# Batch 0 of a recurrent attention and expert kernel as one listed order of named steps

## The chip, the cores and the metric

The kernel runs on one NeuronCore of a Trainium2 chip. The metric is the device time of one execution in microseconds (us), as the median over several runs. Besides the times there is one execution taken by the hardware profiler. Engines are named as the profile names them: PE is TensorE (matmuls and transposes; PEld its weight loads), ACT is ScalarE (activations and copies), DVE is VectorE (elementwise work, reductions, 32x32 transposes), POOL is GpSimd, and SP is the queue that issues most DMAs. All arithmetic is in float32.

## The reference, cut

```python
B, H, S, Ns, D = 8, 8, 512, 32, 64          # d_model = H*D = 512, d_ff = 2048
scale = 1.0 / np.sqrt(D)
scores = scale * np.matmul(x, state.transpose(0, 1, 3, 2))    # tokens x states
a = softmax(scores)                                           # over the states
xread = np.matmul(a, state)
scores2 = scale * np.matmul(state, x.transpose(0, 1, 3, 2))   # states x tokens
a2 = softmax(scores2)                                         # over the tokens
sread = np.matmul(a2, x)
t = concatenate([xread, sread], axis=2), as rows of 512       # 8 * (512+32) rows
h = t @ w_in
sp = np.maximum(h, 0.0) + np.log1p(np.exp(-np.abs(h)))        # softplus
out = (h * erf(sp)) @ w_out
```

`softmax` stands for the subtraction of the maximum, the exponential and the division by the sum plus 1e-9. Both softmaxes use the same products of a state row and a token; only the direction of the maximum and the sum differs.

## The kernel before, in words

The token rows of `xread` are never built. For a batch, `m` = state times `w_in` per head is formed ("mixed"), and `h` = `m` transposed times `aT`, the attention weights with tokens in the free dimension. `d_ff` is cut into four groups of 512 (g = 0 to 3), each into four tiles of 128.

**Batch 0** is a hand-written sequence, because the weights arrive while it runs. `attention0` (line 297) loads `x` in natural layout, transposes it on PE (`turn`, line 308), and copies it to `xT`. The scores are then formed twice: in token layout against a block-diagonal copy of the states, `bd` (`score`, L329), and in state layout (L375). In token layout the softmax over 32 states is a reduction along the free dimension (`less`, `total`, `shared`), followed by transposes (L346) to `aT`. In state layout the softmax over tokens is `rest()` (lines 405 to 415), whose steps are taken one by one later. `warm(n)` (L194) issues n products of the identity that nothing reads.

Weights come in as raw words in 16 pieces, eight of `w_in` (kind i) and eight of `w_out` (kind o), through a pool of three `raw` buffers (line 151). A piece is converted by two ACT instructions (`on_act`, L167 and L169) and three DVE ones (`on_dve`, L172, L173, L174). After the last of them `fetch()` issues the load of the next piece. So the DVE steps set when loads start. Piece i0 is converted in two halves.

For each group, `mixed_part` (L529) forms m, `first0` (L905) h, `soft` and `erf` (L909, L912) are the two activations, `times` (L916) multiplies, and `project` (L700) accumulates the second product into four PSUM banks over all groups. In PSUM there are eight banks: two named `at`, two named `h`, and `o0` to `o3`. `states` (L210) transposes the states of batches 1 to 7. Near its end batch 0 also does the scores, softmax and mixed states of batch 1 (`attention(1)` L427, `mixed`).

**Batches 1 to 7** run in 14 stages n, each two groups of one batch. In a stage the h of one pair of groups is formed by a seven-product scheme (`hidden_wide`, L633) with pieces of the previous stage's second product between, then `project_wide` (L775) follows. Stage n = 0 is batch 1's first; it finishes batch 0's second products (eight of 64) and stores the rows. `excursion` (line 1154) is work for the next batch within a stage: the state read (`read_tokens`, L282), the next m (`mixed_pair`, L512), and the next batch's scores (L232) into the two `h` banks with their copies (L242).

**What sets the order.** Within an engine the instructions keep the order in which the program traces them: `in_order` (line 81) ties each instruction to the one before it on its engine. Between engines semaphores carry the data dependencies, which go by tile and, in PSUM, by bank. DMAs on SP are issued in traced order too; an issue waits until its buffer is free.

Of the kernel before, what the change touches and what calls it, by code (L numbers as in the profile page):

```python
# [17 lines left out]
def kernel(  # L18
# [17 lines left out]
    nc = tc.nc  # L36
# [168 lines left out]
    def states(bs, name):  # L205


        ps = ps_o.tile([P, len(bs), P], F32, name=name)
        for k, b in enumerate(bs):
            nc.tensor.transpose(out=ps[:, k], in_=st[:, b, :], identity=ident)  # L210
        return lambda: nc.scalar.copy(st[:, bs[0]:bs[-1] + 1, :], ps)

# [12 lines left out]
    def scored(b, xT, pool=ps_at, name="at"):  # L225


        s2 = [pool.tile([P, S], F32, name=name) for _ in range(2)]
# [44 lines left out]
    def read_tokens(b, a2T, z2, pool=ps_at, name="at"):  # L273
# [4 lines left out]
        for e in range(2):  # L278
            for c in range(NC):
                for i in reversed(range(NI)):  # L280
                    q = slice(Ns * i, Ns * i + Ns)
                    nc.tensor.matmul(out=sr[q, e, :], lhsT=a2T[:, e, c, q],  # L282
                                     rhs=xt[:, c, 2 * i + e, :],
                                     start=(c == 0), stop=(c == NC - 1))
        sn = sn_t[b] = const.tile([P, 2, D], F32, name="sn0") if b == 0 else \
            st[:, b - 1, :].rearrange("p (e d) -> p e d", e=2)
        for e in range(2):
# [9 lines left out]
    def attention0():  # L297

        xT = att.tile([P, H, 2, P], F32, name="xT")
        xp = [ps_o.tile([P, 2, 2, P], F32, name="o%d" % i) for i in range(NI)]
        bd = away0[:, 0:512].rearrange("p (h k n) -> p h k n", h=H, k=2)
        A = away0[:, 1024:2048].rearrange("p (g c q n) -> p g c q n", g=2, c=NC, q=NI)
        nc.vector.memset(bd, 0.0)
        on = lambda i: (nc.scalar.copy, nc.vector.tensor_copy)[i % 2]

        def turn(i, ks=range(2)):
            for k in ks:
                for e in range(2):  # L310
                    nc.tensor.transpose(
                        out=xp[i][:, e, k],
                        in_=x0[:, 2 * i + e, 2 * k:2 * k + 2].rearrange("p c d -> p (c d)"),
                        identity=ident)

        def keep_x(i):
            on(i)(xT[:, 2 * i:2 * i + 2], xp[i])

        tm, tp, aT[0] = {}, {}, keep.tile([P, 2, S], F32, name="aT")
        m1, z1 = (small.tile([P, 2, NC * NI], F32, name=n) for n in ("m1", "z1"))  # L320
        a = [A[:, g].rearrange("p c q n -> p (c q) n") for g in range(2)]
        tt = nc.vector.tensor_tensor

        def score(g, hs):
            if g not in tm:
                tm[g] = ps_at.tile([P, NC, NI, Ns], F32, name="at")
            for h in hs:
                for k in range(2):
                    nc.tensor.matmul(out=tm[g][:, 2 * k:2 * k + 2, where[h][1]],  # L329
                                     lhsT=xT[:, h, k], rhs=bd[:, h], start=True, stop=True)  # L330

        def less(g):
            t = tm[g].rearrange("p c q n -> p (c q) n")
            nc.vector.reduce_max(out=m1[:, g], in_=t, axis=AX.X)
            tt(a[g], t, over(m1[:, g]), op=ALU.subtract)
            nc.scalar.activation(out=a[g], in_=a[g], func=ACTF.Exp, scale=scale)

        def total(g):
            nc.vector.reduce_sum(out=z1[:, g], in_=a[g], axis=AX.X)
            inverse(z1[:, g])  # L340

        def shared(g):
            tt(a[g], a[g], over(z1[:, g]), op=ALU.mult)
            tp[g] = ps_o.tile([P, S], F32, name="o%d" % g)
# [982 lines left out]
```

## Time and profile before

| | |
|---|---|
| median of 3 runs | 723.47 us (723.39 to 724.16) |
| the profiled execution | 724.1 us, span 722.3 us |
| batch 0 ends, first `hidden_wide` product starts on PE | 111.42 us |
| stage n = 0, its state read starts on PE | 130.71 us |
| its `project_wide` starts on PE | 135.40 us |
| granted TensorE clock, mean | 0.999 |

Busy time of the engines in stretches of 20 us, as the view by windows gives it (stretch, length, then busy us and number of instructions of each engine, the granted clock, the DMA share and GB/s):

```profile
core 0: us, PE busy (x) PEld busy (x) DVE busy (x) ACT busy (x) POOL busy (x), PEclk, DMA share, GB/s
0.00:20.00 20.00, 18.53 (x187) 17.34 (x188) 11.39 (x23) 10.71 (x17) 0.69 (x6) 1.00 0.79 240
20.00:40.00 20.00, 19.63 (x79) 8.04 (x78) 16.16 (x19) 19.20 (x25) 0.00 (x0) 1.00 0.64 211
40.00:60.00 20.00, 19.82 (x90) 8.28 (x90) 16.24 (x19) 19.70 (x23) 0.00 (x0) 1.00 0.79 261
60.00:80.00 20.00, 20.00 (x66) 8.83 (x65) 14.09 (x20) 16.67 (x25) 0.00 (x0) 1.00 0.72 171
80.00:100.00 20.00, 20.00 (x165) 8.09 (x164) 16.64 (x25) 16.71 (x27) 0.00 (x0) 1.00 0.81 199
100.00:120.00 20.00, 18.63 (x70) 9.86 (x69) 17.23 (x27) 11.65 (x18) 0.00 (x0) 1.00 0.83 322
```

PE is busy almost throughout; from 20 to 60 us ACT is as well. A row of the timeline reads: start, duration, engine, line, operation, tiles out and in, shape, number of instructions, and in brackets the idle time before it with what ended it. A matmul's end is modelled, so the distance between two starts says more than its duration. A float32 matmul shows as two instructions, a transpose as one.

### The profile page before, as it was taken

Reading aid. Unit: us, or ns where it says so; the run is one execution under the profiler, and the core shown is the slowest. Engines: PE = TensorE matmul, PEld = TensorE weight load, DVE = VectorE, ACT = ScalarE, POOL = GpSimd, SP = SyncE. Lnnn points to the kernel's source line nnn. Section 1 sums busy time; section 2 is a strip of 40 time slices with the busy share of each in tenths; the row PEclk is TensorE's granted clock in tenths of the full one; section 3 lists DMA queues with packets and bytes.
Section 4 is the critical chain, followed back from the end, with each engine's and each line's share of the span. In section 5 each row is a group of like instructions: output and inputs, shape, how many; then the busy total and the mean of one; then the engine's idle time right before and its main releaser. Section 6 shows DMA issues by size and latency. Waiting matters only on the chain.

```text
span 722.3 us, 10976 instructions
## 1 busy us (share of the span) xinstructions
PE 714.6 (99%) x4289; PEld 565.5 (78%) x4289; DVE 538.2 (75%) x866; ACT 373.1 (52%) x540; POOL 25.2 (3%) x34
## 2 busy tenths in 40 slices
PE   9999999999999999999999999999999999999997
PEld 8444436588878878887888878887888888889996
DVE  5787879889868988788776967697877757665533
ACT  4999784636464625545346436462464535342340
POOL 0000000000100000000000000000000000000000
PEclk9999999999999999999999999999999999999999
DMA  8667795660348153513623280615242321002101
GB/s 266 193 220 211 231 273 180 148 178 30 46 89 217 21 130 55 140 51 92 98 29 147 59 140 8 175 28 148 31 103 84 89 49 27 33 29 30 24 8 30
DMA packets 144341, 74.73 MB, mean 103 GB/s; under 512 B 123424, under 2 KB 132896, under 8 KB 142752
## 3 DMA queue, kind: packets, MB, share of 16 engines
q1 hardware_dynamic: 139520, 65.95, 32.8%
q0 software_dynamic: 4032, 7.34, 7.5%
q10 hardware_dynamic: 736, 0.72, 0.3%
q8 instruction: 34, 0.56, 0.3%
q14 instruction: 19, 0.16, 0.1%
HBM read 49.87 MB, written 20.45 MB: 97 GB/s over the span
## 4 chain that ended last, share of the span: by engine, by line
PE 94%; ACT 3%; DMA 1%; DVE 0%; issue 0%; SPq 0%; ACTq 0%
PE o L775 47%; PE h L633 13%; PE at L633 10%; PE o L700 6%; PE h L678 3%; PE o L750 3%; PE h L905 2%; PE h L512 2%; PE at L512 2%; PE at L282 1%; PE h L232 1%; PE at L905 1%; PE at L529 1%; DMA x<-in_x_dram 1%; PE h L194 1%; PE at L329 1%
## 5 line engine op out<-in xcount | busy, mean ns | idle before, releaser
L775 PE MATMUL o<-w_out,ring 128*128 128x256 f32 x896 | 203.0, 379 | 0.0
L775 PEld LDWEIGHTS o<-w_out,ring 128*128 128x128 f32 x896 | 169.8, 190 | 25.0 <-DVE ring L1139 1.0
L775 PE MATMUL o<-raw,ring 128*128 128x256 f32 x672 | 161.4, 381 | 0.0
L775 PEld LDWEIGHTS o<-raw,ring 128*128 128x128 f32 x672 | 126.5, 190 | 25.9 <-ACT m L514 5.0
L626 ACT ACTIVATE ring<-ring 128x512 f32<-128x512 f32 x112 | 70.6, 631 | 59.9 <-DVE ring L616 59.3
L633 PE MATMUL h<-aT,m 128*128 128x256 f32 x336 | 82.0, 380 | 0.0
L1139 DVE TENSOR_TENSOR ring<-ring 128x1024 f32<-128x1024 f32 x60 | 70.6, 1218 | 3.9 <-ACT ring L690 3.9
L633 PEld LDWEIGHTS h<-aT,m 128*128 128x128 f32 x336 | 63.7, 190 | 10.4 <-issue 0.7
L616 DVE TENSOR_TENSOR ring<-ring,at 128x512 f32<-128x512 f32 x84 | 57.1, 680 | 16.9 <-PE at L633 15.2
L700 PE MATMUL o<-w_out,ring 128*128 128x512 f32 x128 | 58.8, 598 | 1.6 <-DVE ring L916 1.6
L760 DVE TENSOR_TENSOR ot<-uv,o 128x256 f32<-128x256 f32 (+1 forms) x56 | 30.9, 552 | 30.4 <-PE o L775 28.4
L616 DVE TENSOR_TENSOR ring<-ring,h 128x512 f32<-128x512 f32 x56 | 38.0, 678 | 19.7 <-PE h L633 19.6
L798 ACT COPY ot<-o 128x256 f32<-128x256 f32 x28 | 10.4, 373 | 79.6 <-PE o L775 79.6
L836 POOL DMA_DIRECT2D out_dram<-ot x28 | 24.5, 943 | 657.6 <-DVE ot L760 579.8
L700 PEld LDWEIGHTS o<-w_out,ring 128*128 128x128 f32 x128 | 23.7, 190 | 29.9 <-issue 24.4
L760 DVE TENSOR_TENSOR ot<-ot,o 128x256 f32<-128x256 f32 x56 | 22.1, 416 | 27.9 <-ACT ot L798 27.7
L648 ACT COPY ring<-h 128x512 f32<-128x512 f32 x28 | 16.5, 588 | 47.9 <-PE h L633 47.9
L807 DVE TENSOR_TENSOR ring<-ring 128x512 f32<-128x512 f32 x56 | 38.6, 689 | 1.4
L808 DVE TENSOR_TENSOR ring<-ring 128x512 f32<-128x512 f32 x56 | 36.3, 684 | 0.0
L639 ACT COPY ring<-h 128x512 f32<-128x512 f32 x28 | 16.5, 588 | 28.3 <-PE h L633 28.3
L690 ACT ACTIVATE ring<-ring 128x2048 f32<-128x2048 f32 x16 | 30.4, 1902 | 0.0
L514 ACT COPY m<-h 128x512 f32<-128x512 f32 x11 | 6.4, 586 | 44.4 <-PE h L512 44.3
(183 smaller groups left out, 975.6 us busy)
## 6 DMA issues: line engine op xcount, KB each, us to landing
w_in<-kept_in SPq DMA_DIRECT2D x7, 2048.0 KB, 8.2
raw<-in_moe_w_in_dram SPq DMA_DIRECT2D x16, 512.0 KB, 5.6
raw<-in_moe_w_out_dram SPq DMA_DIRECT2D x8, 1024.0 KB, 4.7
out_dram<-ot SPq DMA_DIRECT2D x32, 256.0 KB, 2.2
xq<-in_x_dram SPq DMA_DIRECT2D x112, 64.0 KB, 2.5
x<-in_x_dram SPq DMA_DIRECT2D x56, 128.0 KB, 2.9
out_dram<-ot POOLq DMA_DIRECT2D x28, 256.0 KB, 4.4
sc<-xT SPq DMA_DIRECT2D x112, 32.0 KB, 1.9
```

Source lines behind the costliest of these rows:

```text
L512: nc.tensor.matmul(out=ps[k][e][q, :], lhsT=st[r, b, q], rhs=of_group[g][r, :, i, :], start=True, stop=True)
L616: add = lambda o, x, y: nc.vector.tensor_tensor(o, x, y, op=ALU.add)
L626: nc.scalar.activation(out=s[k], in_=hs[k], func=ACTF.Softplus)
L633: nc.tensor.matmul(out=out[:, i], lhsT=x[:, q:q + P], rhs=y, start=(first and i == 0), stop=(i == 1), skip_group_check=not first)
L690: nc.scalar.activation(out=s, in_=s, func=ACTF.Erf)
L700: nc.tensor.matmul(out=acc[r], lhsT=gT[:, i, P * r:P * r + P], rhs=w_out[:, GF * g + i, :], start=(g == 0 and i == 0), stop=(g == NG - 1 a ...
L760: add = lambda o, x, y: tt(o, x, y, op=ALU.add)
L775: nc.tensor.matmul(out=out, lhsT=lhs[:, i, :], rhs=rhs[:, g, i, :], start=(start and i == 0), stop=(i == GF - 1), skip_group_check=not start)
L807: return [lambda: tt(S1, A21, A22, op=ALU.add), lambda: tt(S2, S1, A11, op=ALU.subtract), lambda: tt(S3, A11, A21, op=ALU.subtract), lambd ...
L808: lambda: tt(S3, A11, A21, op=ALU.subtract), lambda: tt(S4, A12, S2, op=ALU.subtract)]
L836: nc.gpsimd.dma_start(out=rows[2 * h + r][:, c], in_=ot[:, c], accum_op=ALU.add)
L1139: nc.vector.tensor_tensor(s[:, ks], s[:, ks], hs[:, ks], op=ALU.mult)
```

## The change

`attention0`, `first0`, `mixed_part`, `mixed` and the sequence of calls are replaced by a table `do` of named steps and one string that lists them. Three functions fill the table: `start0` (attention of batch 0), `groups0` (m, h, activations and second products) and `weights0` (the conversions); `next0` holds what batch 0 does for batch 1.

How to read the names: `x1` transposes tile 1 of x; `x1_v` and `x3_a` are its copy on DVE or ACT. `st` turns batch 0's states, `s0` and `s1` are the two halves of the scores in state layout, `s00_a` to `s11_a` their copies, `tm0`, `tm1` turn them to token layout; `max`, `less`, `exp`, `sum`, `inv`, `norm` are the softmax over states, `ta` its transposes. `big`, `wt`, `wz`, `wn`, `tw`, `read` are the softmax over tokens and the state read. `i0a0` is ACT step 0 of piece i0 (`+` its second half), `i0v2` a DVE step, `get` loads the next piece. `m10` is m of group 1 from tile 0, `m100_v` its copy; `h11` h of group 1, tile 1 (`h000`: one half of it); `soft`, `erf`, `mul` follow, and `p120` is the second product of group 1, rows 2, tile 0. `u0`, `u1` turn the other states. `lxq`, `lx` load inputs, `q`, `qm`, `qe`, `qs`, `qr`, `n`, `cm`, `ca` are batch 1's scores, softmax, m and sums, and `kept` writes the converted weights to memory.

What differs in the work itself: the scores in token layout are transposes of those in state layout and no longer products with `bd`; the token weights are divided by their sums before their transposes and no longer after the read; `warm(16)` is `warm(12)`; many copies of m are on DVE; the activations of group 1 to 3 come in another grouping with other work between; loads are issued by `get` and no longer by the last conversion step. In stage n = 0 the inner `erf` is issued between the two mixed states, both copies of one bank pair are on two engines, two of the four stores come later, and the products' multiplication is cut in two. From batch 3 on the scores go to the two `o` banks that the next `project_wide` will use.

```diff
+        def turn_st():
+            held["st"] = ps_h.tile([P, 2 * P], F32, name="h")
+            for g in range(2):
+                nc.tensor.transpose(out=held["st"][:, P * g:P * g + P],
+                                    in_=st0[:, g].rearrange("p k d -> p (k d)"), identity=ident)
+
+        def score(g):
+            if not nat:
+                nat.update({k: ps_o.tile([P, 2, 2, P], F32, name="o%d" % k) for k in range(2)})
+            for h in range(4 * g, 4 * g + 4):
+                q = slice(Ns * where[h][1], Ns * where[h][1] + Ns)
+                for c in range(NC):
+                    r = slice(D * (c % 2), D * (c % 2) + D)
+                    nc.tensor.matmul(out=nat[c % 2][q, g, c // 2],
+                                     lhsT=st00[r, Ns * h:Ns * h + Ns], rhs=xT[r, h, c // 2],
+                                     start=True, stop=True)
+
+        def turn_score(g):
+            tm[g] = ps_at.tile([P, NC, NI, Ns], F32, name="at")
+            for c in range(NC):
+                nc.tensor.transpose(out=tm[g][:, c].rearrange("p q n -> p (q n)"),
+                                    in_=sc[:, g, c], identity=ident)
...
+            do["wn%d" % e] = lambda e=e: nc.vector.tensor_scalar(
+                a2[:, e], a2[:, e], z2[:, e:e + 1], None, op0=ALU.mult)
...
+    order0 = """
+        w8 x1 x1_v i0a0 i0a1 x0 x0_v i0v0 i0+a1 i0+a0 st st_v i0v1 x2 x2_v x3 x3_a s0 s00_a i0+v0
+        i0v2 s1 i0+v1 i0+v2 s01_a s10_a tm0 max0 less0 s11_a tm1 exp0 w12 max1 less1 sum0 i1a0
+        inv0 norm0 exp1 o0a0 m01 sum1 m011_a u0 m010_a i1a1 ta0 ta0_a inv1 norm1 m00 ta1 big1
+        i1v0 m000_a get i1v1 i1v2 m001_a h000 ta1_a h01 u0_v o0v0 m02 m020_v h001 u1 m021_v h03
+        h02 o1a1 o0a1 soft01 o0v1 o0v2 u1_v lxq1 soft00 erf00+ mul00 mul01 p030 get o1a0 p020
+        o1v0 o1v1 o1v2 soft03 get p000 soft02 erf02+ mul02 i2a0 mul03 p001 i2a1 p010 i2v0 p031
+        i2v1 i2v2 p021 i3a0 i3a1 i3v0 p002 p011 get p003 o2a1 big0 big p032 o2a0 wt0 m10 m100_v
+        p012 wt1 p013 m101_v h11 soft11 h10 soft10 i3v1 i3v2 m12 m121_a xq1v wz p033 p022 wn0
+        p023 o2v0 m120_v h13 o2v1 o2v2 h12 erf10+ mul10 get o3a1 wn1 get mul11 o3a0 o3v0 o3v1
+        p110 soft13 soft12 o3v2 p111 erf12+ mul12 i4a0 i4a1 get get i5a0 p100 p101 p130 p131 p132
+        mul13 tw0 tw0_a i4v0 i5a1 i4v1 i4v2 p102 p112 m20 m201_a m200_a p120 i5v0 i5v1 p121 p122
+        h20 i5v2 o4a0 o4v0 get m22 m221_v m220_v get h21 o4a1 o4v1 o4v2 tw1 tw1_v h22 soft20 o5a0
+        o5v0 h23 p133 p123 o5a1 soft21 erf20 mul20 erf21 soft23 soft22 o5v1 mul21 p103 erf22 p200
+        o5v2 p201 p220 get erf23 mul22 mul23 i6a0 i6v0 i6a1 i6v1 read read_v p113 i7a0 i7v0 i6v2
+        p210 get get q q1_v p221 p230 qm1 o6a0 q0_a qm0 m30 o6v0 p222 o6a1 m301_v i7a1 p211
+        m300_a o6v1 o6v2 n1 n10_a n11_v qm7 cm0 h30 n0 n01_a i7v1 qm6 h31 lx1 soft31 soft30 p202
+        p203 i7v2 qm8 erf30 n00_v kept cm2 cm1 cm3 m32 m320_a p223 p231 p232 mul30 qm2 erf31 p233
+        p330 m321_a qe3 h33 qm3 mul31 lxq2 o7a0 qm4 o7v0 get get p331 h32 qe2 qm5 p300 p301 qe1
+        qs1 qe0 qs0 p320 p321 qs2 qr0 qr2 soft33 erf33 p212 qr1 p213 p310 p311 o7a1 ca0 qr3
+        soft32 erf32 ca2 mul33 ca1 ca3 o7v1 o7v2 get mul32
+    """
+    steps0 = order0.split()
+    for n, name in enumerate(steps0):
+        if n == len(steps0) - 40:
+            overlap = traced()
+        do[name]()
...
-            (nc.vector.tensor_copy if both and not k else nc.scalar.copy)(m_t[b, g][:, 0], ps[k][0])
+            nc.scalar.copy(m_t[b, g][:, 0], ps[k][0])
             (nc.vector.tensor_copy if split and not k else nc.scalar.copy)(m_t[b, g][:, 1], ps[k][1])
...
+            if k == 0:
+                then()
...
             if c is not None:
-                soft[c] = attention(c, xq_t[c].rearrange("p i m d -> p i (m d)"), ps_h, "h")
+                k = 2 * (n_acc[0] % 2)
+                banks = (ps_h, ("h", "h")) if n == 0 else (ps_o, ("o%d" % k, "o%d" % (k + 1)))
+                soft[c] = attention(c, xq_t[c].rearrange("p i m d -> p i (m d)"), *banks)
...
-        erf_part(inner, inside)
         if n == 0:
             done(steps)
-            excursion(1, (1, sets(1 - begins(1))), 2)
-        times_part(inner, outside)
+            excursion(1, (1, sets(1 - begins(1))), 2, lambda: erf_part(inner, inside))
+            for r in 2, 3:
+                do["put%d" % r]()
+        if n == 0:
+            times_part(inner, slice(0, 1))
+            times_part(inner, slice(3, 4))
+        else:
+            erf_part(inner, inside)
+            times_part(inner, outside)
         times_part(inner, inside)
```

## The prediction

> **What bounds the kernel now.** I read the page's busy shares first, then the list of waits, then the timeline of TensorE where batch 0 starts, where it ends, and where the third and fourth states are mixed.
>
> ```profile
> PE 714.6 (99%) x4289; PEld 565.5 (78%) x4289; DVE 538.2 (75%) x866; ACT 373.1 (52%) x540; POOL 25.2 (3%) x34
> PE 94%; ACT 3%; DMA 1%; DVE 0%; issue 0%; SPq 0%; ACTq 0%
> PE o L700 <- DVE ring L916: 1.6, 2, 1.4
> PE h L194 <- POOL ident masks.py:199: 1.4, 1, 1.4
> ```
>
> TensorE is the bound and nearly never idle, so a gain is either TensorE work that goes, or time that TensorE loses to others. The list of waits admits some 3 us of loss. It understates, because the end of a matmul is modelled: a late operand shows as a row whose instructions stand too far apart. So I compare start times.
>
> ```profile
> 1.36 3.79 PE L194 MATMUL h<-ident 128*128 128x128 f32 x16 [1.36 <-POOL ident masks.py:199]
> 8.49 3.76 PE L329 MATMUL at<-ring,xT 128*128 128x64 f32 x32
> 12.18 2.48 PE L375 MATMUL o<-xT,ring 64*32 64x128 f32 x64
> 14.59 3.84 PE L194 MATMUL h<-ident 128*128 128x128 f32 x32
> 18.26 0.60 PE L346 MATMUL o<-ident,ring 128*128 128x128 f32 x4
> 29.16 7.03 PE L700 MATMUL o<-w_out,ring 128*128 128x512 f32 x16
> 36.38 3.70 PE L700 MATMUL o<-w_out,ring 128*128 128x512 f32 x8 [0.19 <-DVE ring L916]
> 40.27 0.67 PE L529 MATMUL at<-w_in,ring 64*32 64x256 f32 x16 [0.18 <-DVE w_in L174]
> 49.48 9.61 PE L700 MATMUL o<-w_out,ring 128*128 128x512 f32 x22
> 59.02 0.66 PE L529 MATMUL at<-ring 64*32 64x256 f32 x16
> 85.61 2.04 PE L232 MATMUL at<-xq,st 64*32 64x512 f32 x16
> 87.58 1.98 PE L905 MATMUL h<-aT,m 128*128 128x512 f32 x4
> 98.27 3.60 PE L700 MATMUL o<-w_out,ring 128*128 128x512 f32 x8
> 103.23 1.99 PE L700 MATMUL o<-w_out,ring 128*128 128x512 f32 x4 [1.37 <-DVE ring L916]
> 105.15 1.09 PE L529 MATMUL at<-w_in,st 64*32 64x512 f32 x16
> 133.67 1.69 PE L232 MATMUL h<-xq,st 64*32 64x512 f32 x16
> 135.40 1.99 PE L775 MATMUL o<-w_out,ring 128*128 128x256 f32 x8
> 209.93 1.24 PE L232 MATMUL h<-xq,st 64*32 64x512 f32 x16
> 211.10 7.17 PE L775 MATMUL o<-w_out,ring 128*128 128x256 f32 x32
> ```
>
> From 49.48 to 59.02 stand 22 instructions, 0.434 us each: the undisturbed price (a float32 product is two). At 29.16 the 24 take 11.11 instead of 10.41: 0.7 lost. At 98.27 the 12 take 6.88 instead of 5.21: 1.67 lost. State scores take 1.17 undisturbed (209.93 to 211.10); at 85.61 they take 1.97 (0.8 lost), at 133.67 1.73 (0.56 lost). From 135 on every row stands at its price: the change can win nothing there.
>
> Two rows show who releases the start:
>
> ```profile
> 9.15 0.67 ACT L167 ACTIVATE w_in<-raw 128x512 f32<-128x512 f32 x1 [0.40 <-DMA raw<-in_moe_w_in_dram]
> 25.54 1.28 ACT L912 ACT_TABLE_LOAD   x1
> ```
>
> The first weights land at about 9.13, and ScalarE was already waiting.
>
> **What the Trainium skill says.** "TensorE: Matmul & The Clock Gate", section "What's actually happening": the array runs at half clock until it has been busy for some 3.4 us, and again after an idle window of that length. The trace agrees on the first half: the 16 warm-up products at 1.36 take 3.58 us to the next row (0.22 each), the 32 at 14.59 take 3.67 (0.115 each). No row shows a fall back. The same page, "Architectural detail", calls the ScalarE and VectorE queues strict FIFO: a step behind a late one is late too. "PSUM — Partial Sum Buffer", section "PSUM bank collisions raise a hardware error", says to guard by bank and not by address; in the changed program the copy of one half of the natural scores indeed waits for the end of both halves. "ScalarE: Activation LUTs", "What ACT_TABLE_LOAD costs": 1.28 us plus a drain of 1.38. The trace has the 1.28, but the next activation starts at 26.83, right behind the load; I use 1.28.
>
> **The change, part by part.**
>
> *TensorE work.* The 32 score instructions of L329 (3.69 us, 8.49 to 12.18) become 8 transposes of the natural scores (0.11 each by the 8 at 79.39, 0.87 us): 2.8 less. The filler warm(16) becomes warm(12): 8 of 32 instructions, 0.9 less. So 3.7 us of work goes, but all of it lies before 19 us, where TensorE waits for the softmax chain anyway (that is why the filler stood there). It counts only if the chain gets shorter.
>
> *The start, as queues.* The listed order puts four weight conversions ahead of the copies. ScalarE: i0a0 waits for the landing, 9.15 to 9.82, then i0a1, i0+a1 (second half lands about 10.5), i0+a0 to 11.78, then x3_a to 12.27. VectorE: i0v0 waits for i0a0 and st_v stands behind it, ending 10.6. So the first natural scores s0, possible at 8.5 before, start at 10.65; half of 2.41 each, s0 ends 11.85. Copy s00_a (0.37, row L367's size) ends 12.54; s1, which writes its bank, runs 12.6 to 13.8; three more copies to 14.9 (a copy starts some 0.2 behind the matmul, as in all rows); transposes tm0, tm1; max0 15.0 and less0 to 16.4 (0.69 each), exp0 to 17.1, less1 17.7, exp1 behind i1a0 18.65, norm0 19.5, sum1, inv1, norm1 21.3. ta1 and its copy end at 22.6. First product h000 stands at 22.0, against 19.71 before (L905), with m01 and u0 (0.38 + 0.53) already done.
>
> *Up to group 0's second products.* VectorE then does big1 and the three steps of i1 (0.69 + 1.23 + 1.23) to 25.1; m02 waits for them, then h001, u1, h03, h02 (0.6 + 0.87 + 0.33 + 1.75 + 1.75) end at 30.5. On ScalarE i1a1, two copies, o1a1, o0a1, a table load, two softplus, a table load and the erf end at 29.85; mul00 behind u1_v ends at 30.55. p030 starts at 30.6, where the old p started at 29.16: 1.4 late.
>
> *30 to 53.* Seven p (0.87 each) reach 36.6; mul02 is ready at 36.35 (o1a0, two loads, softplus and erf to 35.65). The 0.7 lost before at 29 to 40 is thus gone. m10 waits for i2v2 at 40.25, 0.25 lost. From there the sum of the list is: group 1's first p at 53.0, where the old kernel, at the same state (group 0 done, all h of group 1 done), stood at 52.06. So 0.95 behind.
>
> *53 to the end of batch 0.* The work left is the same. At each step I set the operand beside TensorE: mul12 57.3 for 58.15, i4v2 61.2 for 61.3, mul20 ahead by 3 us, i6v2 1.4 ahead of m30, n00_v 0.6 ahead of m32, combine_a 2 us ahead of the next stage. None is late by this sum; two are within 0.1. Added on ScalarE: five table loads more up to there (21 against 16, 6.4 us), hidden since ten copies of m (0.38 each) move to VectorE and ScalarE was free for about 3 of each 20 us after 60; without that cover each load costs 1.28. Added on VectorE: two scalings wn0, wn1 (0.42 each) for the two of L288. lxq1's 16 issues now stand on SP ahead of i2's load (0.53 each, 17 to 25.5); i2 lands by 32 and is used at 35.5. kept is issued earlier, and the 12 us of its landing no longer meet the next stage. Old stretch 52.06 to 111.42 = 59.36; less 0.8 (scores) and 1.67 (erf wait) gives 56.9; I add 0.45 for read and q standing apart and for products broken into smaller runs: 57.35. Batch 0 ends at 110.35, 1.07 earlier.
>
> *Third stage.* Before, both copies of the first mixed state were VectorE's (132.92 and 133.53, to 134.2) and the scores waited for the second. Now one is ScalarE's, ahead of the inner erf: the scores start as before and lose nothing, 0.56 gained. times(0) alone is ready 0.5 ahead of the first product. The last two puts go behind the score copies; their banks are o2, o3, the next product's o0, o1.
>
> *Scores in the o banks.* No row after 135 loses anything: 0. The banks are last read by the product before; if that cover failed, a wait of one copy (0.59) a stage.
>
> Sum: 1.07 + 0.56 = 1.63, say 1.65. Of the profiled run, 724.1 (span 722.3 and 1.8 around it), 722.45 is left; of the median 723.47, **721.8**.
>
> **Rivals.**
> *The start loses nothing* (group 1's p at 52.06 again, as the copies and landings run ahead of my sum): 0.95 more, and up to 0.3 of edges: 720.6. For: four of the steps are within 0.1 us of TensorE, so the list fits. Against: the landing at 9.13.
> *The ties break the wrong way*: i4v2 for m20, mul12 for p132, n00_v for m32 each some 0.5 late, since five more table loads stand on ScalarE: about 1.5 back, 723.3, no change.
> *The array's clock falls back* (slower). TensorE now idles 8.5 to 10.65 and is half idle to 15.5. If one window counts as idle, s0, s1 and the transposes run at half clock, 1.2 + 1.2 + 0.2 later on the chain, and warm(12) takes 5.3 instead of 2.6 and holds up ta0, 1.4: 4.0 in all, 725.8. It decides where the idle stretch gets beyond 3.4 us by the page; the sum has 2.15.
>
> **How the numbers follow.** Forecast 0.52, start without loss 0.24, ties 0.14, clock 0.10. Two runs of this kernel tell about 0.2% apart, 1.45 us: faster is below 722.0. Of the forecast's own spread (720.6 to 723.0) some 0.58 lies there: 0.30; with the first rival 0.24 and a little of the ties, 0.55. Slower is the clock and little else, 0.10; the rest, 0.35. Range 719.8 to 724.6: below, the first rival with 0.8 for copies moved at nothing; above, ties with one more table load.
>
> **What would show it.** Natural scores starting at 10.6 and h at 22 on TensorE; second products of group 0 at 30.6; no gap in their rows; the old gap of 1.4 at 103 gone; hidden products of the third stage (old 111.42) at 110.35; scores there in 1.2 us. Wrong if the first rows of TensorE after 8.5 stand at double spacing, if m20 or m32 wait, or if rows after 135 change.

## The result, and the profile after

| | before | after |
|---|---|---|
| median of 20 runs each | 724.11 us (723.23 to 724.74) | 722.90 us (721.52 to 725.67) |
| profiled execution, its span | 724.10, 722.3 us | 722.23, 720.4 us |
| batch 0 ends (first product of `hidden_wide`) | 111.42 us | 110.07 us |
| `project_wide` of the third stage starts | 135.40 us | 133.21 us |
| the last group of eight matmuls starts | 716.19 us | 714.68 us |

The ratio of after to before is 0.9985, with a 95% interval of 0.9978 to 0.9992: a gain of about 1.1 us (0.6 to 1.6), small but clear of zero. The runs of the changed kernel also spread over 4.2 us, those before over 1.5.

The small sum hides larger parts. The timeline of TensorE after the change, with start, busy time, the group and the idle time ahead of it:

```profile
9.64 0.72 PE L788 MATMUL o<-xT,ring 64*32 64x128 f32 x32 [2.29 <-DVE ring L748]
11.66 1.16 PE L788 MATMUL o<-xT,ring 64*32 64x128 f32 x32 [1.30 <-ACT ring L747]
14.94 4.25 PE L194 MATMUL h<-ident 128*128 128x128 f32 x24
19.12 0.45 PE L877 MATMUL at<-w_in,ring 64*32 64x128 f32 x16
21.86 2.84 PE L887 MATMUL h<-aT,m 128*128 128x512 f32 x6 [0.17 <-ACT m L747]
30.26 9.68 PE L894 MATMUL o<-w_out,ring 128*128 128x512 f32 x22
39.87 0.67 PE L877 MATMUL at<-w_in,ring 64*32 64x256 f32 x16
61.23 0.67 PE L877 MATMUL at<-ring 64*32 64x256 f32 x16 [0.39 <-DVE ring L174]
103.20 7.03 PE L894 MATMUL o<-w_out,ring 128*128 128x512 f32 x16
110.07 1.03 PE L489 MATMUL h<-aT,m 128*128 128x256 f32 x4
132.04 1.24 PE L224 MATMUL h<-xq,st 64*32 64x512 f32 x16
133.21 1.99 PE L631 MATMUL o<-w_out,ring 128*128 128x256 f32 x8
150.06 1.03 PE L489 MATMUL h<-aT,m 128*128 128x256 f32 x4
152.75 1.13 PE L489 MATMUL h<-aT,m 128*128 128x256 f32 x4 [1.66 <-DVE ring L472]
```

Read it by start times, as before. The 22 second products from 30.26 to 39.87 take 9.61, their price (0.437 each); the 0.7 that the old kernel lost there is gone. So is the wait of 1.67 at 98 to 105: from 103.20 the 16 products run through. The scores of the third stage take 1.17 (132.04 to 133.21) in place of 1.73. But at 150.06 there is something that the old kernel did not have: four hidden products that should take 0.86 take 2.69, until 152.75. From there to the end the changed kernel is 1.25 us shorter than the old one at the same work.

The sum, on the start times of TensorE: batch 0 -1.35, third stage -0.84, fourth stage +1.93, later stages -1.25, together -1.51; another 0.4 of the span lies behind the last matmul, and no run asks why. Of these four the forecast had the first two.

### The new wait

From the view of waits of the changed kernel, the new one of TensorE (what waited, for whom, us in total, times, longest):

```profile
PE h L489 <- DVE ring L472: 1.7, 1, 1.7
```

What VectorE did in front of that L472 (two rows of the softmax, between 149.56 and 151.36, are left out):

```profile
143.17 1.30 DVE L321 STREAM_TRANSPOSE xT<-sc 128x512 f32<-128x512 f32 x2
147.77 0.69 DVE L616 TENSOR_TENSOR ot<-uv,o 128x512 f32<-128x512 f32 x1 [3.30 <-PE o L631]
148.37 1.27 DVE L323 TENSOR_REDUCE m<-xT 128x16 f32<-128x512 f32 x2
151.36 0.74 DVE L616 TENSOR_TENSOR ot<-ot,o 128x256 f32<-128x256 f32 x2
152.02 0.68 DVE L472 TENSOR_TENSOR ring<-ring,h 128x512 f32<-128x512 f32 x1
```

It stood still for 3.30 us before the add into an output buffer `ot` at 147.77. The view names a product (PE o L631), the releaser that came last by its records. But this add takes the first eight of the 24 products that start at 142.29, and they end at their price by 144.0. What else does the add need? The buffer `ot`, one of three, and its last reader is a store. SP's queue, before the change and after it (first issue, length, what is issued, how many):

```profile
133.32 0.82 SPq L838 DMA_DIRECT2D out_dram<-ot  x2
134.23 4.53 SPq L75 DMA_DIRECT2D x<-in_x_dram  x8
138.88 9.11 SPq L102 DMA_DIRECT2D xq<-in_x_dram  x16
```

```profile
130.35 5.09 SPq L75 DMA_DIRECT2D x<-in_x_dram  x8
135.55 8.46 SPq L102 DMA_DIRECT2D xq<-in_x_dram  x16
144.12 1.85 SPq L694 DMA_DIRECT2D out_dram<-ot  x2
```

Before, the last two stores of batch 0 went out at 133.32, ahead of the 24 loads that the excursion brings. After, they are traced behind the excursion and go out behind its 24 issues: 144.12. Each lands 3.5 us after its issue, the first at about 147.65, and the add starts at 147.77. (That SP issues in traced order is tied only in batch 0: the last `in_order`, for the stages behind it, names TensorE, VectorE and ScalarE. There the trace has to show the order, as here.) That the one causes the other is argued from times so far; the first experiments test it.

### The profile page after: what moved, and what is told of

Same layout as the page of the kernel before. It is cut to its first block, busy times and chain, and to the rows that moved or that the text cites. A ratio compares the mean times of both kernels' runs of the same rounds, so it can differ in the third digit from the quotient of the medians.

```text
span 720.4 us, 10904 instructions
## 1 busy us (share of the span) xinstructions
PE 708.6 (98%) x4257; PEld 561.2 (78%) x4257; DVE 542.0 (75%) x877; ACT 374.8 (52%) x535; POOL 25.2 (3%) x34
## 4 chain that ended last, share of the span: by engine, by line
PE 89%; ACT 4%; DMA 2%; SPq 2%; DVE 2%; issue 1%; DVEq 0%; ACTq 0%
PE o L631 46%; PE h L489 13%; PE at L489 10%; PE o L894 5%; PE h L534 3%; PE o L606 3%; PE h L383 2%; PE at L383 1%; PE at L275 1%; SPq L102 1%; PE h L887 1%; ACT raw L169 1%; PE at L887 1%; DMA raw<-in_moe_w_in_dram 1%; DMA raw<-in_moe_w_out_dram 1%; SPq L75 1%
## 5 line engine op out<-in xcount | busy, mean ns | idle before, releaser
L631 PE MATMUL o<-w_out,ring 128*128 128x256 f32 x896 | 203.0, 379 | 0.0
L631 PEld LDWEIGHTS o<-w_out,ring 128*128 128x128 f32 x896 | 169.9, 190 | 24.8 <-DVE ring L1089 0.8
L631 PE MATMUL o<-raw,ring 128*128 128x256 f32 x672 | 161.4, 381 | 0.0
L631 PEld LDWEIGHTS o<-raw,ring 128*128 128x128 f32 x672 | 126.6, 190 | 25.8 <-ACT m L385 9.2
L1089 DVE TENSOR_TENSOR ring<-ring 128x1024 f32<-128x1024 f32 (+1 forms) x61 | 70.6, 1200 | 4.5 <-ACT ring L546 4.5
L472 DVE TENSOR_TENSOR ring<-ring,at 128x512 f32<-128x512 f32 x84 | 57.0, 679 | 16.8 <-PE at L489 15.2
L472 DVE TENSOR_TENSOR ring<-ring,h 128x512 f32<-128x512 f32 x56 | 38.0, 678 | 19.7 <-PE h L489 19.6
L894 PEld LDWEIGHTS o<-w_out,ring 128*128 128x128 f32 x128 | 23.6, 190 | 27.2 <-issue 24.6
L616 DVE TENSOR_TENSOR ot<-ot,o 128x256 f32<-128x256 f32 x56 | 22.1, 416 | 27.9 <-ACT ot L654 27.7
L504 ACT COPY ring<-h 128x512 f32<-128x512 f32 x28 | 16.4, 586 | 47.9 <-PE h L489 47.9
L489 PE MATMUL h<-sy,sx 128*128 128x256 f32 x112 | 28.7, 379 | 0.0
```

The lines of the kernel that those rows point to most:

```text
L472: add = lambda o, x, y: nc.vector.tensor_tensor(o, x, y, op=ALU.add)
L489: nc.tensor.matmul(out=out[:, i], lhsT=x[:, q:q + P], rhs=y, start=(first and i == 0), stop=(i == 1), skip_group_check=not first)
L616: add = lambda o, x, y: tt(o, x, y, op=ALU.add)
L631: nc.tensor.matmul(out=out, lhsT=lhs[:, i, :], rhs=rhs[:, g, i, :], start=(start and i == 0), stop=(i == GF - 1), skip_group_check=not start)
L894: nc.tensor.matmul(out=acc[r], lhsT=gT[g][:, i, P * r:P * r + P], rhs=w_out[:, GF * g + i, :], start=(made_of[r] == 1), stop=(made_of[r] = ...
L1089: nc.vector.tensor_tensor(s[:, ks], s[:, ks], hs[:, ks], op=ALU.mult)
```

## The experiments

All runs are compared with the kernel before on the same chip. Its medians there lie between 724.06 and 724.41 us, so kernels of different groups are compared by their ratios. Every kernel computes the whole output.

### What makes the fourth stage wait

Theory 1: the order on SP. Theory 2: the copies and the erf that the change puts on ScalarE in the third stage. A third is batch 0's list itself. Four kernels ran together.

**e1**, the third stage's edits taken back (the forms of the kernel before: stores at the end of each row of second products, copies of the first mixed state on VectorE, one erf ahead of the excursion, its multiplication in one instruction). 

> The changed kernel with the third stage's edits taken back: all four output blocks of batch 0 are copied and stored ahead of the scores, both copies of the first mixed state are VectorE's, the erf of the inner half stands ahead of the scores, and its multiplication is one instruction. The list of batch 0 and the score banks stay. Theory 1 (the two late stores stand on SP behind the 24 issues of the next loads, so their output buffers come free 12 us late and VectorE's add in the fourth stage waits): the stores land near 136, the wait of 1.7 us in the hidden products near 151 is gone, and the scores near 132 take 1.73 again instead of 1.17; the excess from 130 on falls by about 1.9 - 0.6 - 0.3 = 1.0, and the time is about 722.0, 0.9987 of the changed kernel's. Theory 2 (the wait comes from the copies or the erf on ScalarE): the wait goes too. A third (it comes from batch 0's list, which leaves VectorE more to do): it stays at 1.7, and the time grows by 0.6 to 0.8, to 723.6.

**e2**, only the loads move:

```diff
+            waiting.append(lambda: None)
             excursion(1, (1, sets(1 - begins(1))), 2, lambda: erf_part(inner, inside))
             for r in 2, 3:
                 do["put%d" % r]()
+            all_of(waiting)
+            waiting.clear()
```

where `load_x` and `load_xq` are put into `waiting` while it is not empty. 

> The changed kernel with one difference: in the third stage the loads of the next x and the next turned x are issued behind the two late stores instead of ahead of them; copies, erf and scores stay where they are. Theory 1 (order on SP): the two stores land near 136 instead of 148, VectorE's add with the output buffer o2 waits for nothing, the wait of 1.7 us near 151 is gone, and nothing takes its place, since the loads come only some 1.3 us later: 1.9 us less, 721.0, 0.9974 of the changed kernel's. Theory 2 (copies or erf on ScalarE): the wait stays, 722.9, a ratio of 1.000.

**e3**, only the queue of the two stores changes:

```diff
-            put_x(0, r // 2)(r % 2, ot)
+            put_x(0, r // 2)(r % 2, ot, queue=nc.scalar if r > 1 else nc.sync)
```

> The changed kernel with one difference: the two late stores of batch 0 are issued on ScalarE's queue, each behind its own copy, and SP's order of loads stays. Theory 1: as with the loads behind the stores, the wait near 151 is gone and the time is 721.0 (0.9974); what two issues take on ScalarE (not shown so far, estimated at no more than 0.1 to 0.6 us each, by SP's 0.53 a DMA) stands behind the score copies and hits the erf of the outer half, which has 2 us of room. Theory 2: the wait stays, 722.9 (1.000).

**e5**, e2 with `banks = ps_h, ("h", "h")` for all stages. 

> The loads issued behind the two late stores, as in the run of that name, and besides the scores of all later stages back in the two h banks, as before the change. The forecast said that the o banks change nothing: then this equals the run with the loads behind the stores, 721.0, and the score rows take 1.17 in both. A second reading, from the rows of the changed kernel (0.995 us for a group of 16 in the o banks, 1.165 in the h banks of the kernel before): five groups take 0.17 longer, 0.85 in all, 721.85, ratio 1.0012 to the other.

| | median, us | ratio to before, 95% | wait near 151 | third-stage scores |
|---|---|---|---|---|
| after | 722.90 | 0.9985 (0.9978 to 0.9992) | 1.93 | 1.17 |
| e1 | 721.66 | 0.9968 (0.9955 to 0.9980) | 0 | 1.73 |
| e2 | 720.11 | 0.9952 (0.9940 to 0.9965) | 0 | 1.16 |
| e3 | 720.87 | 0.9959 (0.9947 to 0.9972) | 0 | 1.17 |
| e5 | 721.97 | 0.9975 (0.9968 to 0.9983) | 0 | 1.16 |

SP's queue of e2, and the same add of VectorE there (L622 in its numbering):

```profile
131.57 5.63 SPq L75 DMA_DIRECT2D x<-in_x_dram  x8
137.31 0.44 SPq L102 DMA_DIRECT2D xq<-in_x_dram  x1
137.85 0.91 SPq L700 DMA_DIRECT2D out_dram<-ot  x2
138.81 9.18 SPq L102 DMA_DIRECT2D xq<-in_x_dram  x15
```

```profile
144.38 1.30 DVE L327 STREAM_TRANSPOSE xT<-sc 128x512 f32<-128x512 f32 x2
145.60 0.65 DVE L622 TENSOR_TENSOR ot<-uv,o 128x512 f32<-128x512 f32 x1
```

The stores pass 15 of the 16 issues of `xq` (the eight of `x` and one of `xq` still go first, though traced behind the stores: nothing ties SP's order here), and the add starts right behind the transpose, with no idle time. e3 leaves SP's order and moves only the two stores off it: the wait goes as well. Both leave the copies and the erf on ScalarE where the change put them. Theory 2 is refuted, and theory 1 shown. The third falls with e1, which keeps the list and has no wait. In e3 the two issues took 0.37 and 0.36 on ScalarE's queue, and ScalarE needed 2.09 from the first of the two copies to the next erf, in e2 0.96. 0.47 of that came back as a late product at 144.67. So e2 is the cleaner cure in the trace, though the times of the two can't be told apart. The Trainium skill, "DMA: Bandwidth & Descriptors", section "Issuing engines are not separate DMA queues", says that another queue saves only the issuer's time, usually small beside the transfer. The traces agree on what is saved, but here it wasn't small: the 24 issues ahead of the stores took SP 13.7 us, and a store landed in 3.5.

e1 shows the size of the third stage's edits without their side effect: from batch 0's end to `project_wide` it needs 23.82 us (111.13 to 134.95), e2 and the changed kernel 23.14, the kernel before 23.98. So these edits are worth 0.68 of the third stage's 0.84.

### The score banks

e5 against e2 says that the o banks are worth more than noise: 0.9975 against 0.9952, and in the traces 1.24 us between 165 and the last matmul (by start times, some 0.85 in the five score groups and 0.40 in the mixed states ahead of them). So the part was tried alone on the kernel before. **e11**:

```diff
-                soft[c] = attention(c, xq_t[c].rearrange("p i m d -> p i (m d)"), ps_h, "h")
+                k = 2 * (n_acc[0] % 2)
+                banks = (ps_h, ("h", "h")) if n == 0 else (ps_o, ("o%d" % k, "o%d" % (k + 1)))
+                soft[c] = attention(c, xq_t[c].rearrange("p i m d -> p i (m d)"), *banks)
```

> The kernel before, and of the change only the banks: the scores of the stages behind the third go to the o banks that the next product of outputs will use. The forecast's step: nothing, 723.5 to 724.2. What the comparison of the two score banks in the changed kernel showed (five score rows 0.17 shorter each, mixed states 0.4 shorter in all): 1.2 to 1.3 less than before, 722.9, ratio 0.9982.

It took 722.88 us, ratio 0.9983 (0.9977 to 0.9990), and 1.24 us less between 165 and the last matmul. The reason stands in the view of one line's instructions, which says until when its engine was idle ahead of it. The kernel before, then e11, both for the scores (L232) between 165 and 720 us:

```profile
L232 PE MATMUL h<-xq,st x80: 589/601/614, 209.9 to 498.0; 64*32 64x512 f32 x80
its engine sat idle before it (us, times) until:
  ACT m L514: 3.9, 5
```

```profile
L232 PE MATMUL o<-xq,st x80: 589/589/590, 209.9 to 496.8; 64*32 64x512 f32 x80
its engine sat idle before it (us, times) until:
  issue: 2.8, 10
```

In the h banks every one of the five score groups waits for ScalarE's copy of the mixed state that has just been formed in the same banks. In the o banks nothing holds it. (The us of this view are not the loss: e11 has 2.8 there, and its groups stand closer. The loss is read from start times.) A group of 16 takes 0.995 in the o banks; the 1.17 that stood for its price contained that wait each time.

### The start of batch 0

In the changed kernel the first scores wait until 9.64 (2.29 idle), and the granted clock of TensorE falls. Windows of 3 us (stretch, length, busy us and count of PE, PEld, DVE, ACT, POOL, the granted clock, DMA share, GB/s), before (one stretch) and after:

```profile
12.00:15.00 3.00, 3.00 (x70) 2.73 (x69) 2.61 (x6) 2.41 (x5) 0.00 (x0) 1.00 1.08 368
```

```profile
9.00:12.00 3.00, 1.06 (x48) 0.80 (x56) 2.88 (x7) 2.34 (x5) 0.00 (x0) 0.84 1.10 397
12.00:15.00 3.00, 2.83 (x41) 2.15 (x26) 1.89 (x3) 0.92 (x3) 0.00 (x0) 0.50 1.10 356
15.00:18.00 3.00, 3.00 (x16) 3.00 (x16) 2.86 (x7) 2.21 (x4) 0.00 (x0) 0.52 0.60 101
```

That is the mechanism of the forecast's slower rival. Four kernels, all on e2, ask what it and the start's order cost. **e4** puts `w8 w8` (16 filler products, 32 instructions) between `x3_a` and `s0`. 

> The kernel with the loads behind the two late stores, and 16 more filler transposes between the last transpose of x and the first natural scores, where TensorE idles 2.3 to 3.1 us. Clock theory (that gap lets the granted clock fall to half: 0.50 to 0.55 at 12 to 18 us, against 1.00 in the kernel before): the clock stays at 1.00, the scores take 2.4 in place of 3.1, the eight transposes of the scores 1.0 in place of 2.2, the twelve filler pairs 2.7 in place of 3 to 4.2; the first maximum starts 1 to 1.5 earlier, and the second products of batch 0 start 0.5 to 1 earlier; 719.5. Rival (the queues of ScalarE and VectorE bind there, and the first copy behind the landing of the weights sets the time): the clock rises and the rows get short, but the first maximum and the second products of batch 0 move by less than 0.4; 720.1.

**e7** takes `w12` (24 instructions) out of the list. 

> The kernel with the loads behind the two late stores, and without the filler of 24 transposes between the turned scores and the first mixed state (12 pairs listed as w12). In the changed kernel's profile it took 4.17 us at half clock, to 19.12, and the first transposes of the weights stood 1.2 behind their operand. If the filler holds the chain up at half clock: the first transposes of the weights start at 19.1 to 19.3, the clock is at half until then and beyond, and mixed states and first h take up to twice as long[...]. I expect the two to cancel: second products of batch 0 within 0.5 of the kernel with the filler, 720.1 to 720.6. If the clock is what matters, 721.5 or more.

**e6** lists the copies first:

```diff
-        w8 x1 x1_v i0a0 i0a1 x0 x0_v i0v0 i0+a1 i0+a0 st st_v i0v1 x2 x2_v x3 x3_a s0 s00_a i0+v0
-        i0v2 s1 i0+v1 i0+v2 s01_a s10_a tm0 max0
+        w8 x1 x1_v x0 x0_v st st_v x2 x2_v x3 x3_a i0a0 i0a1 i0v0 i0v1 s0 s00_a i0v2
+        i0+a1 s1 i0+a0 i0+v0 s01_a s10_a i0+v1 i0+v2 tm0 max0
```

> The kernel with the loads behind the two late stores, and the copies of the turned x and of the turned states listed ahead of the first weight conversions. Queue theory, as in the forecast (the copies stand behind a conversion that waits for the landing of the weights at 8.1 to 8.7): the first scores start at about 7.9 in place of 9.6 to 10.2, TensorE's gap is below 1 us, the clock stays at 1.00, the first maximum starts at 12.6 in place of 14.3 to 14.7, the first h near 20.3 in place of 21.7. What follows of it: if ScalarE is next bound by the landing of the second piece of w_out (22.1 and 23.6 in two traces; its conversion stands ahead of the first softplus), the second products of group 0 still start near 30.3, and the time stays within 0.5 of 720.1; if not, they start 1.5 earlier, 718.7.

**e8** is e6 with `o1a1` behind `erf00+` and `p120` ahead of `m20`. 

> The kernel with the early copies and two more moves in the list: the first half of the conversion of the second piece of w_out stands behind the first erf in place of ahead of the first softplus, and one pair of second products (p120) stands ahead of the mixed state m20, which waited 0.4 to 0.8 for the conversion of a piece of w_in. If the landing of that piece of w_out binds ScalarE: the first softplus starts when both h are there (near 22.5) and not behind the landing, and the second products of group 0 start at 28.7 to 29.3, 1.2 to 2 earlier; the wait at 59 falls from 0.45 to below 0.1; 718.0 to 718.6. If VectorE's conversions bind instead, the second products start within 0.4 of the other kernels' 30.3, and only the 0.4 at 59 goes: 719.7.

| | weights land | clock at half, us | first erf ends | second products start | batch 0 ends | between | median, us; ratio (95%) |
|---|---|---|---|---|---|---|---|
| before | 9.1 | never | | 29.16 | 111.42 | 82.26 | |
| after | 8.11 | 11.05 to 17.9 | 29.39 | 30.26 | 110.07 | 79.81 | 722.90; 0.9985 |
| e2 | 8.70 | 12.3 to 15.7 | 30.69 | 31.55 | 111.28 | 79.73 | 720.11; 0.9952 (0.9940 to 0.9965) |
| e4 | 9.66 | never | 30.72 | 31.59 | 111.78 | 80.19 | 721.47; 0.9961 (0.9949 to 0.9974) |
| e7 | 8.94 | 10.0 to 23.6 | 30.43 | 31.30 | 110.77 | 79.47 | 720.71; 0.9946 (0.9932 to 0.9959) |
| e6 | 8.13 | 19.9 to 23.3 | 29.56 | 30.43 | 110.53 | 80.10 | 720.81; 0.9950 (0.9937 to 0.9962) |
| e8 | 8.58 | never | 28.54 | 29.41 | 111.49 | 82.08 | 721.25; 0.9956 (0.9944 to 0.9968) |

The clock is read from windows of 0.5 us. In all six kernels behind the first row the second products start 0.86 or 0.87 us behind the end of the first erf: ScalarE's queue sets their start.

The times of e2, e4, e6 and e7 can't be told apart. e7, at half clock for longest, has the lowest ratio, and e4, never at half, the highest. So the half clock occurred, and no cost of it shows in the times; one below about 1 us would not show in runs that spread like these. e4 tests less than it was meant to. Its filler ends at 12.50 and the scores start right behind it, though VectorE's copy of the turned states, which lets them start in the changed kernel and in e2, ended at 11.14; its weights also landed 0.96 later than e2's. The first maximum, expected 1 to 1.5 earlier, came at 15.67 against 14.71. No run changes the clock alone.

e6 did on the chip what the queue argument says: scores at 7.74 in place of 10.23 in e2, the first maximum at 12.74 in place of 14.71. Yet its second products start within 0.2 of the changed kernel's. ScalarE waited 0.77 for the second piece of `w_out` (until 22.60), with the first softplus behind that conversion. And the half clock came after all, later: TensorE idled 2.63 at 16 us, waiting for the load of the other states. The same six hidden products in e6, then in e8 at full clock:

```profile
21.00 3.90 PE L893 MATMUL h<-aT,m 128*128 128x512 f32 x6
```

```profile
21.05 2.84 PE L893 MATMUL h<-aT,m 128*128 128x512 f32 x6
```

They take 1.07 longer in e6 (3.84 and 2.77 to the next row), and TensorE's rows show no idle time from there to 30.43. So ScalarE and TensorE were ready there almost together. e8 moved the conversion, kept its clock, and got 29.41, just outside the 28.7 to 29.3 expected; with e6's clock TensorE would not have been ready before some 30.2 (estimated from e8's own rows, 29.2, and the 1.07). Then it lost all of it:

```profile
29.41 6.25 PE L900 MATMUL o<-w_out,ring 128*128 128x512 f32 x14
36.14 3.70 PE L900 MATMUL o<-w_out,ring 128*128 128x512 f32 x8 [0.49 <-DVE ring L930]
40.27 0.67 PE L883 MATMUL at<-w_in,ring 64*32 64x256 f32 x16 [0.42 <-DVE w_in L174]
59.03 1.12 PE L900 MATMUL o<-w_out,ring 128*128 128x512 f32 x2 [0.80 <-DVE ring L930]
```

The next multiplication (36.14), the next piece of weights (40.27) and the last multiplication of group 1 (59.03) are late in turn. Three rows of ScalarE in e8 say why:

```profile
31.91 1.09 ACT L923 ACTIVATE ring<-at 128x512 f32<-128x512 f32 x2
38.16 1.17 ACT L167 ACTIVATE w_in<-raw 128x1024 f32<-128x1024 f32 x1 [0.47 <-DMA raw<-in_moe_w_in_dram]
41.32 1.17 ACT L169 ACTIVATE raw<-raw 128x1024 uint32<-128x1024 uint32 x1 [0.91 <-DMA raw<-in_moe_w_out_dram]
```

The second pair of softplus starts at 31.91 in e6 as well: the moved conversion stands ahead of it in both, so the multiplication behind it is no earlier in e8. At 38.16 and 41.32 ScalarE waits for pieces of weights, 0.47 and 0.91 (0.18 and 0.20 in e6), and from there to the last erf of group 1 it runs 1.2 behind e6.

How little room ScalarE has in this stretch is seen in the view by windows, from 22 to 57 us, of the changed kernel (fourth of the busy times is ScalarE's):

```profile
22.00:57.00 35.00, 34.89 (x126) 14.74 (x127) 31.48 (x41) 34.53 (x39) 0.00 (x0) 1.00 0.72 207
```

In the changed kernel ScalarE is busy for 34.53 of 35 us, in the kernel before for 33.92, in e8, with its waits, for 32.42. The reading that led to the next run was that a full ScalarE pushes back whatever stands behind a moved conversion. To test it, **e9**, which is e8 with one more move, takes a table load out of this stretch: the token weights' exponentials of batch 0 go to 21 us, where the exponential's table is still loaded.

```diff
-        h02 ... p011 get p003 o2a1 big0 big p032 o2a0 wt0 m10 m100_v
-        p012 wt1 p013
+        ... ta1 big1 big0 big wt0 i1v0 m000_a ... h000 ta1_a wt1 h01 ...
```

> The kernel of the last group with the early copies, and the two exponentials for the token weights of batch 0 beside the two of the state weights (their maximum right behind big1), so that one load of the exponential's table at 43.6 goes (1.28 us of ScalarE), and 1.8 us of exponentials move from 45 to 20 to 22. Theory: from 22 to 57 ScalarE is the bound of the list (busy 34.5 of 35 us in the changed kernel), and takes back what an earlier start gives. Then the second products of group 0 start later than 29.4, near 30.6, but the waits behind them (1.0 at 36, 0.5 at 40, 1.0 at 57) go, and batch 0 ends near 110.1 in place of 111.5: 719.6 to 720.2. Rival (VectorE or the landings bind this stretch): the waits stay, and the later start comes on top: batch 0 ends at 112 or later, 721.8.

**e10** is e2 with `p120` ahead of `m20` alone. 

> The kernel with the loads behind the two late stores, and one pair of second products (p120) ahead of the mixed state m20. The wait of 0.4 to 0.8 us at 59 to 60 (for VectorE's last step of a piece of w_in) goes, since 0.87 us of other work stands there; all else stays: 0.4 less, 719.8. If the wait moves to the next step of the list instead, the time is that of the kernel without the move, 720.2.

**e12** is e10 with e6's order of copies. 

> The kernel with the loads behind the two late stores, with the early copies (second products of group 0 at 30.4, batch 0's end at 110.5 in their own run, 0.8 of it lost at 59 to 60) and with p120 ahead of the mixed state m20 (which took away that loss in its own run). If the two add up: batch 0 ends at 109.7, and the time is 719.9 to 720.3, 0.9942 of the kernel before. If ScalarE, as in the runs before, gives an earlier start back later in the list: batch 0 ends at 110.3 to 110.6, 720.6, as each of the two alone.

| | second products start | batch 0 ends | between | median, us; ratio (95%) |
|---|---|---|---|---|
| e9 | 30.47 | 111.23 | 80.76 | 721.60; 0.9973 (0.9966 to 0.9981) |
| e10 | 30.55 | 110.39 | 79.84 | 720.67; 0.9956 (0.9942 to 0.9969) |
| e12 | 30.03 | 109.86 | 79.83 | 720.92; 0.9960 (0.9946 to 0.9973) |

e9 is half a hit: it starts at 30.47 as expected and the wait at 59 is gone, but 0.6 at 36 and 0.4 at 40 stay, and batch 0 ends only 0.26 earlier than in e8, not 1.4. ScalarE was not alone there: it now idles 1.42 and 1.12 us at 45 to 47, waiting for products. So ScalarE's queue sets the start of the second products, and behind that landings and several engines bind in turn; which of them could be relieved stays open. In e10 the wait at 59 to 60 is gone (in e6 it cost 0.78, in e2 0.47), but it has moved: the scores in batch 0, at 80.78, take 1.46 in place of the 1.02 of e2, and from second products to batch 0's end it needs what e2 needs. e12 ends batch 0 at 109.86, the earliest of all, only because it starts at 30.03; its expected 0.9942 lies just outside its interval. All kernels with the loads behind the stores and the scores in the o banks beat the kernel before by 2.5 to 4.0 us, and all but e9 lie beyond the changed kernel's interval too. Which of them is best these runs can't say.

## Why the prediction came out as it did

The forecast was 721.8 us, for a gain of 1.65; the medians give 1.2 and the profiled executions 1.9. It gave 0.55 to a time below 722.0, and the median stayed above. Of the 1.1 us between 721.8 and 722.90, 0.64 is the base: it was taken from three runs, 723.47, where twenty give 724.11. That the gain came so near is luck in part. Batch 0 and the third stage gave 2.19 in the profile for 1.63 forecast, and two things that the sum had at nothing, 1.93 lost and 1.25 won, partly cancelled.

**Right: TensorE's lost time as the ledger.** The losses named beforehand went where forecast: 0.7 at 29 to 40, 0.8 at the scores of batch 0 (1.02 for the group in place of 1.97), 1.67 at 103, and 0.56 at the third stage's scores, which got 0.84 shorter in all. Batch 0 ended at 110.07 for a forecast of 110.35. One part of that sum held by luck: from group 1's first second product to the end it allowed 0.45 beyond 56.9, for broken runs; 0.65 came (52.52 to 110.07), and 0.56 of it is the tie below.

**Right in the number, not in the steps: the start.** The sum gave first h at 22.0 and second products at 30.6; measured 21.86 and 30.26. But the weights landed at 8.11, a microsecond earlier than assumed, and the half clock took most of what that gave: the filler took 4.18 us (14.94 to 19.12) and held the first mixed state and the transposes of the weights behind it. The landing differs from execution to execution: 8.11 to 9.66 in the profiles here. The bank guard acted as the sum had it, and not as the paragraph on the skill says: the second half of the scores waits for the copy of the first (11.66, behind ACT L747), and that copy does not wait for both halves.

The slower rival thus came true in its mechanism, though it was to decide only beyond an idle stretch of 3.4. Between 7.35, when the transposes of x end, and 11.66 TensorE worked 0.72 us, in gaps of 2.29 and 1.30; the clock fell at 11.05, 3.7 us after 7.35. The Trainium skill's "TensorE: Matmul & The Clock Gate", section "What's actually happening", speaks of an idle window of about 3.4 us. The traces here do not agree: no single gap is that long, and in e7 the clock fell at 10.0, when TensorE had idled for 1.7 since its transposes of x. Nor does the length of a gap decide: after 2.63 idle at 16 us e6 fell at 19.9, and after 2.64 there e8 did not. What failed in the rival was the price of 4.0. Against e6's rows at full clock the second half of the scores took 0.44 more, the eight transposes 0.47 and the filler 1.40, 2.3 in all, for the first half still ran at full clock; and the earlier landing paid for part of it.

**In part: the ties.** Of the three pairs that the second rival named, one broke, m20 for i4v2: 0.56 us (58.96 to 61.23, four products and the wait). The other two held.

**Wrong, the step that failed: "The last two puts go behind the score copies; their banks are o2, o3, the next product's o0, o1."** It looked at the PSUM banks alone. A put is also a store on SP and an output buffer in SBUF, of which there are three. The excursion that it was moved behind issues 24 loads, 13.7 us of SP, and the next user of the buffer is an add in VectorE's queue, with the hidden products of the fourth stage behind it. The step had the cost of that wait at nothing. Measured: 1.93 us in the profile, and e2 and e3 get it back. The issues of `lxq1` were counted past SP in batch 0, but not these.

**Wrong, in the other direction: "No row after 135 loses anything: 0", for the score banks.** The price of a score group, 1.17, was read from rows that all had the same wait inside. The view of that line's instructions shows it, "ACT m L514: 3.9, 5", in the trace of before. Worth 1.24 us of TensorE's time, as e5 and e11 show from both sides.

Taken off the median, 722.90 - 1.93 + 1.25 = 722.2: an estimate of what the priced parts alone would have given, a gain of 1.9 on 724.11 for a forecast of 1.65.

## What to carry to other kernels

When a step is moved, list every resource that it holds to its end (bank, buffer, queue, transfer) and what it is moved past on each queue: a store that slips behind 24 loads frees its buffer 11 us later, and whoever needs that buffer waits on another engine, under another name. The undisturbed price of an operation is not the shortest row of a kernel if all its rows have the same neighbour: ask what each waits for before taking it as the floor. And an earlier start is worth only what the next queue lets through: here the first erf on ScalarE, and behind it the landings.

## What the runs showed of the hardware

- The granted clock of TensorE halved 3.7 us after dense work ended, though 32 small matmuls (0.72 us) had run in between, and came back at 17.9 us; the filler of 24 instructions then took 4.18 us in place of the 2.78 of e6 (12.15 to 14.93). In e7 it halved 1.7 us after that work, in e2 5.0. Gaps of 2.63 and 2.64 at the same place were followed by half clock in e6 and by none in e8.
- SP needed 8.46 us for 16 issues of 64 KB and 5.09 for eight of 128 KB, 0.53 and 0.64 each. Two stores issued from ScalarE's queue took 0.37 and 0.36, and each left a gap of 0.44 behind the copy that it follows.
- A group of 16 score products took 0.995 us in the o banks, where nothing held it, and 1.17 in the h banks, where each group waited for ScalarE's copy of the mixed state.
- The load of the first weights landed between 8.11 and 9.66 us in these profiled executions of nearly the same first transfers. Where ScalarE waited for the second piece of `w_out`, it came between 22.1 (e12) and 23.6 (e2).
